# Chunked state-space scan with a gated feed-forward block: the second half of each chunk's y on exchanged PSUM column halves, copied out by two engines

## The chip, the cores and the metric

The kernel runs on one core of a Trainium2 chip. Its time is device microseconds of one launch; lower is better. The core has a matrix engine (TensorE, PE in the profile, its weight loads PEld), VectorE (DVE), ScalarE (ACT), GpSimd (POOL) and a queue engine that issues DMAs (SyncE, SP). They run side by side and wait for one another through semaphores. Each engine works through its instructions in program order. TensorE writes its results into PSUM; ScalarE and VectorE copy them from there into SBUF.

## What is computed

The reference is a chunked state-space scan (Mamba-2 style), followed by a feed-forward layer with the activation h·sigmoid(1.702·h). The core of the scan, per chunk:

```python
L = np.exp(cum[:, :, :, None] - cum[:, :, None, :]) * causal
M = np.einsum('bhin,bhjn->bhij', Cc, Bc) * L
y_intra = np.einsum('bhij,bhjd->bhid', M, xc)
y_inter = np.einsum('bhin,bhnd->bhid', Cc, state) * decay_to_i[:, :, :, None]
y[:, :, sl] = y_intra + y_inter
state = decay_full[:, :, None, None] * state + np.sum(Bx, axis=2)
...
h = x @ w_in                               # x is y, 3072 tokens x 256
out = (h / (1 + np.exp(-1.702 * h))) @ w_out   # 256 -> 2048 -> 256
```

There are 4 batches, 8 heads, 768 positions, 32 values per head and a state of 16 per head, all in fp32 on the chip.

## The kernel before

**Tiling.** The 3072 tokens are worked in six groups of 512 (numbers 0 to 5 in the code, "group one" to "group six" in the text). A group is four chunks of 128 positions, taken as two pairs of chunks. Each chunk of 128 is again two halves of 64 positions; the loop variable `i` is the half, `k` the chunk within a pair, `n` the pair.

**Making y.** `finish` computes y for a group in two steps. `inter` (line 821) multiplies the carried states with C: for each half `i` and each of four row strips `r` of 32 rows (two heads each), one matmul of 32 rows by 64 columns. `intra` (line 833) multiplies the masked, decayed scores with x: for each head and half one matmul of 64 rows by 32 columns, the half `i` choosing the upper or lower 64 rows. The position of a matmul on the array of 128 rows and 128 columns is `tile_position`; its columns are also the PSUM partitions of its result. Each fp32 matmul is two instructions in the profile, so a group has 128 of line 833 and 64 of line 821, or 56 where a batch begins in it and one state is zero.

The result is `y`, four PSUM banks: one for each half `i` and each tile `t` of 128 features (four heads of 32). The first group (`early`) has its own four banks and its own copies; groups two to six share one area of four banks (`area`, tag "cb", one buffer) with the scores `cb` and with the accumulators `acc`. That area is handed on in program order: scores, then y, then `acc` of the same round.

**Copying y.** ScalarE copies the two halves into `yT` in SBUF (line 860), with 128 partitions and 512 elements each.

**Using y.** `yT` of group two is used at once: `project_all(0)` computes the first group's output, with `finish` of group two between its steps, and `hidden(1, ...)` (line 889) follows. The later groups' `yT` is used a round later: `mix_y` (lines 913 to 915, VectorE) mixes its halves, since from group two on the feed-forward products are done by a seven-product scheme (Strassen-like): `first` (lines 945 to 955) for the first layer with PSUM results X and Y, copied and added by ScalarE (line 950) and VectorE (line 1077) into gT; `mix_g` mixes gT, and `product` (line 1050) accumulates the second layer in `acc`.

**Order.** All of it is one program written out by hand: strings such as `"2.T y refill 3.D 4.1 4.5 4.2 3.4 P P 4.6 P"` name the steps of a round in order, where `y` stands for `finish`, `3.D` for an addition on VectorE, `4.1` to `4.7` for products of the first layer and `P` for one of the second. `in_order` at the end fixes this order on each engine. `refill` sets off the loads for a later pair. `spread` (line 256) is the one of them that brings `a`, spread over the partitions, for the VectorE scan `decay` (line 402); it may be held back by a small memset on VectorE (line 253), behind which its DMAs stand on SP's queue.

Of the kernel before, what the change touches and what calls it, by code (L numbers as in the profile page):

```python
# [11 lines left out]
AF = mybir.ActivationFunctionType  # L12
# [23 lines left out]
def kernel(  # L36
# [31 lines left out]
    nc = tc.nc  # L68
# [4 lines left out]
    NB, NH, S, D = x.shape  # L73
# [5 lines left out]
    HB = NH // 2  # L79
# [7 lines left out]
    Q = NH // R  # L87
    H = P // 2
# [191 lines left out]
    early = const.tile([P, 1], FP32, name="early")  # L280
# [99 lines left out]
    for i, n, head in ((0, 1, PG), (1, 2, PG), (0, 0, 1)):  # L380
        t = whose[32 * i:32 * i + 32, n:n + 1]
# [14 lines left out]
    yT = {}  # L396
# [184 lines left out]
    def bank(name):  # L581
        return ps.tile([P, 4 * P], FP32, tag="ff", name=name)

    def area(name):
        return psa.tile([P, R, 4 * P], FP32, tag="cb", name=name)
# [202 lines left out]
    def finish(pairs, steps=range(2)):  # L788


        g, first = divmod(pairs[0], PG)
        early = pairs[0] < PG
        if 0 in steps:
            if early:
                y = [bank(f"y0_{i}")[:, :2 * P].rearrange("p (k i) -> p k i", i=H) for i in range(4)]
                begun_y[0] = [[y[2 * t + i] for t in range(NK)] for i in range(2)], set()
            else:
                both = area(f"y{pairs[0]}")[:, :, :len(pairs) * 2 * H].rearrange(
                    "p (s t) (k i) -> p s t k i", s=2, i=H)
                begun_y[pairs[0]] = [[both[:, i, t] for t in range(NK)] for i in range(2)] + [both], set()  # L800
        y, begun = begun_y[pairs[0]]

        def begin(i, t, parts):
            new = not begun & {(i, t, q) for q in parts}
            begun.update((i, t, q) for q in parts)
            return new

        def inter(n, p, ts=range(2)):

            for k in range(2):  # L810
                for i in range(2):
                    m = 2 * k + i
                    if (4 * p + m) % (2 * NC) == 0:
                        continue
                    old = state[p][:, m - 1] if m else state[p - 1][:, 3]
                    for r in range(R):
                        t = r // 2
                        if t not in ts:
                            continue
                        rows, to = slice(32 * r, 32 * r + 32), Q * D * (r % 2)  # L820
                        nc.tensor.matmul(  # L821
                            out=y[i][t][to:to + Q * D, 2 * n + k], lhsT=old[rows],
                            rhs=st[p]["CsT"][rows, k, SIDES[i]],
                            start=begin(i, t, range(Q * (r % 2), Q * (r % 2) + Q)), stop=early,
                            tile_position=(32 * r, to), skip_group_check=True)

        def intra(n, p):
            L = Ls[p]
            for k in range(2):
                for h in range(NH):  # L830
                    t, q = divmod(h, HB)
                    for i, side in enumerate(SIDES):
                        nc.tensor.matmul(  # L833
                            out=y[i][t][D * q:D * q + D, 2 * n + k], lhsT=rx[p][side, k, h],
                            rhs=L[side, k, h // Q, h % Q],
                            start=begin(i, t, (q,)), stop=not early, tile_position=(H * i, D * q),
                            skip_group_check=True)

        cols = slice(2 * first * P, 2 * (first + len(pairs)) * P)

        if first == 0:
            yT[g] = ffn.tile([P, NK, TG], FP32, tag="yT", name=f"yT{g}")
        if early:
            for n, p in enumerate(pairs):
                intra(n, p)
            for t in range(NK):
                for n, p in enumerate(pairs):
                    inter(n, p, (t,))
                for i in range(2):
                    nc.scalar.activation(  # L850
                        yT[g][:, t, cols].rearrange("p (k s i) -> p s k i", s=2, i=H)[:, i], y[i][t],
                        AF.Copy)
        else:
            for step in steps:
                for n, p in enumerate(pairs):
                    (inter, intra)[step](n, p)
            if 1 not in steps:
                return
            for i in range(2):
                nc.scalar.activation(  # L860
                    yT[g][:, :, cols].rearrange("p t (k s i) -> p s t k i", s=2, i=H)[:, i], y[2][:, i],
                    AF.Copy)
        for p in pairs:
            state.pop(p - 1, None)
            st.pop(p)
            Ls.pop(p)
# [234 lines left out]
    def turn_out(g, i):  # L1101

        t = out_tile(g, i).rearrange("p k e -> p (k e)")
        nc.vector.transpose(out=t, in_=sums[g][:, i].rearrange("p t e -> p (t e)"))
        rows = out[g * TG:(g + 1) * TG].rearrange("(b j) d -> j b d", j=32)
        for r in range(R):
            cols = slice(i * P + 32 * r, i * P + 32 * r + 32)
            nc.sync.dma_start(out=rows[:, :, cols],
                              in_=t[32 * r:32 * r + 32].rearrange("p (b e) -> p b e", e=32))
# [90 lines left out]
    keep_first()  # L1200
    dense(2)
    finish(range(PG))
    dense(0)
    join(0, 2)
# [25 lines left out]
    for i, k, c in ((2, 1, 1), (3, 2, 2), (4, 4, 4), (5, 6, 8), (6, 9, 12), (7, 12, 15)):  # L1230
# [3 lines left out]
    n, p = 2 * PG, 3 * PG  # L1234
# [7 lines left out]
    at(in_project[0], 9, lambda: score(pairs), lambda: gain(pairs), lambda: keep_both(pairs, True),  # L1242
       lambda: weigh(PG), lambda: weigh(PG + 1))
    at(in_project[0], 13, lambda: finish(pairs, (0,)))
    at(in_project[0], 15, lambda: finish(pairs, (1,)))
    at(in_project[0], 13, lambda: mix_in(1), lambda: mix_in(2), lambda: mix_in(3),
       lambda: turn_blocks(2), lambda: decay(n))
# [86 lines left out]
    k = NF // 2 - 1  # L1334
# [6 lines left out]
    for g in range(2, NG):  # L1341
        n, p = (g + 1) * PG, (g + 2) * PG
        more, most = g + 1 < NG, g + 2 < NG
        rows = [b for b in range(NB) if most and (g + 2) * CG <= b * NC < (g + 3) * CG]
# [32 lines left out]
        if more:  # L1377
# [4 lines left out]
                y=lambda: finish((n, n + 1)), refill=refill,  # L1382
# [6 lines left out]
        for j in range(5 if more else 4, NF // 2):  # L1389
            if j == 5:  # L1390
                do = lambda: (mix_g(g, 3), turn_out(g - 1, 0))
            else:
                do = lambda: mix_g(g, j - 2)
            run(g, steady(j, "o" if j == 6 else ""), seven(g, j - 4), M=do,
                o=lambda: turn_out(g - 1, 1))
# [6 lines left out]
        k = NF // 2 - 1  # L1402
# [42 lines left out]
```

## Time and profile before

| | |
|---|---|
| median of 3 runs | 350.76 us (350.66 to 352.0) |
| profiled execution | 349.68 us, of which 347.8 are the span of the core |
| granted TensorE clock | 1.000 |
| y, line 833 | 768 matmul instructions, median 216 ns each |
| y, line 821 | 352 matmul instructions, median 217 ns each |
| copies of y, line 860 | 10, median 592 ns each |

The span is the time from the first to the last instruction on the core; the rest of the execution lies around it. A line of the timeline gives start and length in us, the engine, the line of the kernel, the operation, the tile written and the tiles read, the sizes, the count of instructions merged into it and, in brackets, how long the engine stood idle before and what ended that. Matmuls overlap, so that the length of one is no measure of how fast they follow one another; that is read from their starts. PEld waits that end in a weight load are the waits of TensorE, because each matmul follows its load.

### The profile page before, as it was taken

The numbers are of one execution on the slowest core, as the hardware profiler recorded it, in microseconds if no ns is written. First come the engines' busy times: TensorE is split into PE (matmuls) and PEld (weight loads), VectorE is DVE, ScalarE is ACT, GpSimd is POOL, SyncE is SP. The second block draws the span as 40 slices with busy tenths as digits, with TensorE's granted clock in tenths as the row PEclk, the third lists the DMA queues.
The fourth block names the chain that finished last, engine by engine and source line by source line (L and its number), as shares of the span: only waits on it lengthen the run. The fifth ranks groups of instructions, "written<-read, shape, count | busy, mean of one in ns | idle before, by whom it ended". The sixth has DMA issues, their size and how long they took to land.

```text
span 347.8 us, 8141 instructions
## 1 busy us (share of the span) xinstructions
PE 342.0 (98%) x3392; PEld 271.9 (78%) x3392; DVE 253.5 (73%) x479; ACT 153.1 (44%) x349; POOL 12.9 (4%) x41
## 2 busy tenths in 40 slices
PE   8899999999999999999999999999999999999996
PEld 6644444557788888888888888888888888899996
DVE  5899999998679998839995649787555654455463
ACT  5698573107354324744332543442444321554320
POOL 8300000000000100000000000000000000000000
PEclk9999999999999999999999999999999999999999
DMA  6699997435526100435613036300000300000301
GB/s 162 142 336 193 283 212 155 81 77 93 105 58 128 33 2 15 63 104 102 101 28 50 2 81 117 64 2 1 2 2 2 61 2 0 0 2 0 62 0 61
DMA packets 89980, 25.92 MB, mean 75 GB/s; under 512 B 73432, under 2 KB 87128, under 8 KB 89944
## 3 DMA queue, kind: packets, MB, share of 16 engines
q1 hardware_dynamic: 89112, 24.88, 33.3%
q10 hardware_dynamic: 832, 0.52, 0.5%
q8 instruction: 26, 0.43, 0.5%
q14 instruction: 10, 0.08, 0.1%
HBM read 22.15 MB, written 3.24 MB: 73 GB/s over the span
## 4 chain that ended last, share of the span: by engine, by line
PE 97%; ACT 1%; DVE 1%; issue 0%; DVEq 0%
PE acc L1050 28%; PE X L945 20%; PE Y L955 14%; PE h L889 10%; PE o L987 8%; PE acc L1057 7%; PE y L833 2%; PE y L821 2%; PE cb L682 2%; PE A L713 1%; PE busy L440 1%; PE ab L554 1%; PE ab L548 0%; DVE steps L735 0%; ACT steps L730 0%; ACT drop L522 0%
## 5 line engine op out<-in xcount | busy, mean ns | idle before, releaser
L950 ACT ACTIVATE ac<-X 128x256 f32<-128x256 f32 x76 | 29.1, 383 | 78.6 <-PE X L945 78.2
L1050 PE MATMUL acc<-mg,mw 128*128 128x256 f32 x192 | 54.5, 379 | 0.0
L922 ACT ACTIVATE gT<-gT 128x512 f32<-128x512 f32 (+1 forms) x76 | 39.3, 520 | 34.1 <-DVE gT L1077 33.4
L1077 DVE TENSOR_TENSOR gT<-Y,ac 128x512 f32<-128x512 f32 x38 | 26.2, 689 | 36.1 <-PE Y L955 30.5
L945 PE MATMUL X<-my,mi 128*128 128x256 f32 x152 | 45.2, 380 | 0.0
L1077 DVE TENSOR_TENSOR gT<-Y,b 128x256 f32<-128x256 f32 x38 | 15.8, 419 | 35.2 <-PE Y L955 35.2
L1050 PEld LDWEIGHTS acc<-mg,mw 128*128 128x128 f32 x192 | 36.5, 190 | 5.0
L1050 PE MATMUL acc<-gT,w_out 128*128 128x256 f32 x128 | 35.5, 379 | 0.0
L889 PE MATMUL h<-yT,w_in 128*128 128x512 f32 (+2 forms) x98 | 35.5, 518 | 0.0
L945 PEld LDWEIGHTS X<-my,mi 128*128 128x128 f32 x152 | 28.0, 190 | 4.1 <-ACT ac L950 0.4
L889 PEld LDWEIGHTS h<-yT,w_in 128*128 128x128 f32 x98 | 17.0, 190 | 16.5 <-issue 14.3
L987 PE MATMUL o<-gT,w_out 128*128 128x512 f32 x64 | 28.6, 597 | 0.0
L913 DVE TENSOR_TENSOR mg<-gT 128x512 f32<-128x512 f32 x40 | 27.2, 681 | 0.0
L1050 PEld LDWEIGHTS acc<-gT,w_out 128*128 128x128 f32 x128 | 24.2, 190 | 3.4 <-ACT yT L860 0.2
L950 ACT ACTIVATE b<-X 128x256 f32<-128x256 f32 x38 | 14.6, 384 | 20.0 <-PE X L945 19.6
L945 PE MATMUL X<-yT,w_in 128*128 128x256 f32 x76 | 23.2, 389 | 0.0
L945 PE MATMUL X<-my,w_in 128*128 128x256 f32 x76 | 22.7, 382 | 0.2 <-issue 0.2
L955 PE MATMUL Y<-yT,w_in 128*128 128x256 f32 x76 | 22.7, 381 | 0.0
L955 PE MATMUL Y<-my,mi 128*128 128x256 f32 x76 | 22.6, 379 | 0.0
L955 PE MATMUL Y<-yT,mi 128*128 128x256 f32 x76 | 22.5, 379 | 0.0
L987 PEld LDWEIGHTS o<-gT,w_out 128*128 128x128 f32 x64 | 11.8, 190 | 13.2 <-issue 12.7
L402 DVE TENSOR_TENSOR_SCAN L<-a,idents 128x1024 f32<-128x1024 f32 x9 | 20.5, 2277 | 0.4 <-DMA a<-scratch 0.4
(156 smaller groups left out, 544.2 us busy)
## 6 DMA issues: line engine op xcount, KB each, us to landing
a<-scratch SPq DMA_DIRECT2D x18, 256.0 KB, 5.3
bits<-in_moe_w_out_dram SPq DMA_DIRECT2D x8, 512.0 KB, 5.4
x<-in_x_dram SPq DMA_DIRECT2D x24, 128.0 KB, 3.0
out_dram<-ob SPq DMA_DIRECT2D x40, 64.0 KB, 1.9
bits<-in_moe_w_in_dram SPq DMA_DIRECT2D x8, 256.0 KB, 4.6
bits<-in_moe_w_in_dram SPq DMA_DIRECT2D x4, 512.0 KB, 9.3
b<-in_B_dram SPq DMA_DIRECT2D x20, 64.0 KB, 3.0
af<-in_a_dram SPq DMA_DIRECT2D x3, 384.0 KB
```

Of the source, the lines that this page charges most:

```text
L402: nc.vector.tensor_tensor_scan(out=L, data0=ra[p].rearrange("p k e -> p (k e)"), data1=idents.rearrange("p h i -> p (h i)"), initial=0.0, ...
L682: nc.tensor.matmul(out=s["cb"][side, r, k].rearrange("p (q i) -> p q i", q=Q), lhsT=BT[rows, k, side], rhs=CT[rows, k, :, side], start=Tru ...
L889: nc.tensor.matmul(out=h[:, cols], lhsT=w_in[:, f, k], rhs=yT[g][:, k, cols], start=(k == 0 and e == 0), stop=(k == NK - 1), skip_group_ch ...
L913: nc.vector.tensor_tensor(out=t[:, 0:2], in0=B[:, :, 1], in1=B[:, 0], op=ALU.subtract)
L922: nc.scalar.activation(o, i, AF.Silu, scale=GELU_SCALE)
L945: nc.tensor.matmul(out=s["X"], lhsT=lhsT, rhs=rhs, start=i == "1", stop=i == "4", skip_group_check=True)
L950: nc.scalar.activation(copy, s["X"], AF.Copy)
L955: nc.tensor.matmul(out=o, lhsT=lhsT, rhs=rhs, start=s.pop("new", False), stop=i != "5", skip_group_check=True)
L987: nc.tensor.matmul(out=o[c], lhsT=w_out[:, c, f], rhs=gT[g, f // 2][:, f % 2], start=(f == 0), stop=(f == NF - 1), skip_group_check=True)
L1050: nc.tensor.matmul(out=acc[g][0][i][:, cols], lhsT=w, rhs=h[:, cols], start=(j == 0 and k == 0 and (i, 0) in begins), stop=(j == NF // 2 - ...
L1057: nc.tensor.matmul(out=o[k] if type(o) is list else o[:, cols], lhsT=h[:, cols], rhs=w, start=(j == 0 and (i, k) in begins), stop=(j == NF ...
L1077: nc.vector.tensor_tensor(out=o, in0=v, in1=w, op=ALU.add)
```

## The change

For groups two to six the second half `i` of each chunk puts its results on the other column half of the array, in both steps. In `inter` the 64 columns of a row strip are those of `r % 2` for the first half of a chunk and of the other value for the second. In `intra` the 32 columns of a head move by two strips for the second half. So in the PSUM banks of the second half, partitions 0 to 63 and 64 to 127 have changed places. The copy puts them back: the first half is copied by ScalarE as before; of the second, VectorE copies partitions 64 to 127 of y to 0 to 63 of yT, and ScalarE partitions 0 to 63 of y to 64 to 127 of yT. The first group (`early`) is as before. Lines after the change are three further down from the copy on.

```diff
@@ inter
                         t = r // 2
                         if t not in ts:
                             continue
-                        rows, to = slice(32 * r, 32 * r + 32), Q * D * (r % 2)
+                        half = r % 2 ^ (not early and i)
+                        rows, to = slice(32 * r, 32 * r + 32), Q * D * half
                         nc.tensor.matmul(
                             out=y[i][t][to:to + Q * D, 2 * n + k], lhsT=old[rows],
                             rhs=st[p]["CsT"][rows, k, SIDES[i]],
-                            start=begin(i, t, range(Q * (r % 2), Q * (r % 2) + Q)), stop=early,
+                            start=begin(i, t, range(Q * half, Q * half + Q)), stop=early,
                             tile_position=(32 * r, to), skip_group_check=True)
@@ intra
                 for h in range(NH):
-                    t, q = divmod(h, HB)
                     for i, side in enumerate(SIDES):
+                        t, q = divmod(h, HB)
+                        if i and not early:
+                            q = (q + Q) % HB
                         nc.tensor.matmul(
                             out=y[i][t][D * q:D * q + D, 2 * n + k], lhsT=rx[p][side, k, h],
@@ the copy
-            for i in range(2):
-                nc.scalar.activation(
-                    yT[g][:, :, cols].rearrange("p t (k s i) -> p s t k i", s=2, i=H)[:, i], y[2][:, i],
-                    AF.Copy)
+            o = yT[g][:, :, cols].rearrange("p t (k s i) -> p s t k i", s=2, i=H)
+            nc.scalar.activation(o[:, 0], y[2][:, 0], AF.Copy)
+            nc.vector.tensor_copy(o[:H, 1], y[2][H:, 1])
+            nc.scalar.activation(o[H:, 1], y[2][:H, 1], AF.Copy)
```

`Q` is 2 (heads per row strip), `D` 32, `HB` 4 (heads per tile of 128 features) and `H` 64.

## Prediction

> **What bounds the kernel now.** I read the page's shares and the chain that ended last first. Then I read the two matmul lines of y, the timeline around each of the five places where a y is made, and last the order of the changed program with the semaphore each instruction waits for.
>
> ```profile
> PE 342.0 (98%) x3392; PEld 271.9 (78%) x3392; DVE 253.5 (73%) x479; ACT 153.1 (44%) x349; POOL 12.9 (4%) x41
> PE 97%; ACT 1%; DVE 1%; issue 0%; DVEq 0%
> ```
>
> TensorE sets the time, at a granted clock of 1.000. What it stops doing is gained and what it waits is lost, unless a later wait takes it back. The state-space part is small: the two matmul lines of y are 2% of the chain each.
>
> ```profile
> 91.58 1.16 PE L821 MATMUL y<-CsT,S 32*64 32x64 f32 x64
> 96.76 1.48 PE L833 MATMUL y<-L,x 64*32 64x64 f32 x128
> 98.39 1.07 ACT L860 ACTIVATE yT<-y 128x512 f32<-128x512 f32 x2
> 99.50 0.73 PEld L1050 LDWEIGHTS acc<-gT,w_out 128*128 128x128 f32 x4 [0.18 <-ACT yT L860]
> 148.53 1.04 PE L821 MATMUL y<-CsT,S 32*64 32x64 f32 x56
> 180.12 0.79 PE L713 MATMUL A<-x,Be 64*32 64x64 f32 x56
> ```
>
> The first four lines are y of group three, its copy and what comes next. The two copies run one behind the other on ScalarE and end at 99.46; 0.04 later TensorE loads for `acc`, which lives in the PSUM area that y leaves. So here the copy has no slack. For groups four and five the copies end at 152.19 and 205.51 and the same load stands at 152.62 and 205.93, about 0.43 later. For group six they end at 258.88 and the load stands at 259.74, because TensorE itself lost 0.34 just before.
>
> **Part 1: `inter`.** Each matmul there uses 32 rows and 64 columns. Before, row strips 0 and 2 always use the left column half and 1 and 3 the right one, so four places of the array work. The records show four starts 6.7 ns apart, then the next four 58 ns after the first four. With the halves exchanged for the second half of a chunk, the eight matmuls of a chunk fall on eight places. The nearest row is L713, which has the same 64 moving columns on eight places: from its first matmul to the next stage it takes 0.72 for 56 (180.12 to 180.84) and 0.79 for 64. L821 takes 0.97 for 56 (148.53 to 149.50) and 1.09 for 64 (91.58 to 92.67). That is 0.25 and 0.30 less; its weight loads are twice as wide, so I take 0.23 and 0.28. Bounds: nothing at one end, half of the 0.83 and 0.94 between first and last start (0.41 and 0.47) at the other.
>
> A rule speaks against this gain. The Trainium skill, TensorE: Matmul & The Clock Gate, section "Wait — 56ns, not 53.3ns?", says that starts never come closer than about 25 ns however small the matmul. By it 56 matmuls would need 1.4 us and the exchange could bring nothing. The starts 6.7 ns apart in this trace contradict it for matmuls on separate places.
>
> **Part 2: `intra`.** It already covers eight places (two row halves, four column strips), and its first 32 starts stand 6.7 ns apart within each eight. The exchange permutes them: 0, bounded by ±0.1 a place, since L833 itself ranges from 1.41 to 1.50 first start to next stage.
>
> **Part 3: the copy.** In before, the second ScalarE copy starts 0.49 after the first (98.39, 98.86) and the pair takes 1.08. In the changed program the VectorE copy waits for a ScalarE semaphore, and the second ScalarE copy waits for a VectorE semaphore. The first copy is the only newer ScalarE work, so the three run strictly in turn. One ScalarE copy of 512 elements lasts 0.59; half the partitions leave the elements per partition alone. The VectorE copy is not in the trace. Its nearest row is L1077, which reads 512 PSUM elements in 0.69; the fast end is L480, VectorE on SBUF, 768 in 0.54, which with L341 (256 in 0.295) gives 0.42 for 512. I take 0.69. Hand-overs between engines measure 0.04 (98.03 to 98.06, 94.22 to 94.26). The chain is 0.59 + 0.04 + 0.69 + 0.04 + 0.59 = 1.95, against 1.08: **0.87 later** (0.60 with the fast copy).
>
> The Trainium skill, VectorE: DVE Perf Modes, section "Mode 2×_2P — use both read ports for one tensor", gives fp32 copies their double rate from SBUF only, since PSUM has one read port. By it the slow end is the right one, and the fast end would take 0.27 off every place.
>
> **What it meets, place by place.**
>
> Group two's first tile of work, `hidden(1, 0)`, needs all of yT. VectorE has the copy behind this queue:
>
> ```profile
> 77.13 2.22 DVE L402 TENSOR_TENSOR_SCAN L<-a,idents 128x1024 f32<-128x1024 f32 x1
> 78.47 1.09 ACT L860 ACTIVATE yT<-y 128x512 f32<-128x512 f32 x2 [11.39 <-PE y L833]
> 79.39 0.49 DVE L461 TENSOR_TENSOR Be<-b,L 128x128 f32<-128x128 f32 x2
> 79.80 2.29 DVE L402 TENSOR_TENSOR_SCAN L<-a,idents 128x1024 f32<-128x1024 f32 x1
> 80.19 3.68 PE L889 MATMUL h<-yT,w_in 128*128 128x128 f32 x24
> ```
>
> VectorE is 9.86 of 10 us busy from 70 to 80. The program puts the copy after `Be` and before the second scan, so it starts at 79.80 however early y is done, and the 0.23 of `inter` buys nothing here. It ends at 80.49, the last ScalarE copy at 81.12, the weight load starts at 81.17; a load that was waited for adds 0.11 (259.42: first matmul spaced 0.32, not 0.21). So 81.28 instead of 80.19: **+1.09**. The scan behind the copy slips 0.6, less than TensorE.
>
> Group three's y (the 98.39 lines): −0.28, then the area comes free 0.87 later. The load stood 0.06 before its matmul and now needs 0.11: +0.91. Net **+0.63**. Behind the copy on VectorE stand the two `mix_g`, and behind those a memset that gates the next DMA of `a` on SP's queue:
>
> ```profile
> 101.01 0.06 DVE L253 MEMSET a<- 128x1 f32 x1
> 101.10 1.27 SPq L256 DMA_DIRECT2D a<-scratch  x2
> 106.87 2.29 DVE L402 TENSOR_TENSOR_SCAN L<-a,idents 128x1024 f32<-128x1024 f32 x1 [0.37 <-DMA a<-scratch]
> 116.72 0.42 ACT L922 ACTIVATE gT<-gT 128x256 f32<-128x256 f32 x1 [2.71 <-DVE gT L1077]
> 117.05 0.37 ACT L950 ACTIVATE ac<-X 128x256 f32<-128x256 f32 x1
> 117.46 0.30 PEld L945 LDWEIGHTS X<-my,mi 128*128 128x128 f32 x2 [0.39 <-ACT ac L950]
> ```
>
> The scan already waits for that DMA; VectorE then works without a gap over 0.6 until 116.69, ScalarE waits for it, and TensorE at 117.46 waits for ScalarE. There is no slack in this row of waits. Before, VectorE began the first `mix_g` at 97.94, 0.30 before y's end at 98.24; now the copy ends 1.46 after y's end (copy one starts 0.15 after it, 0.58, 0.04, 0.69), and the `mix_g` begins 0.08 earlier than that. So the memset, the DMA and the scan slip 0.30 + 1.38 = 1.68 against y. TensorE has slipped 0.91 against y, so at 117.46 it waits another **+0.77**. The cover if I am wrong: a DMA that lands sooner than the 5.7 of before.
>
> Groups four and five's y (151.11 and 204.42): −0.23; the copies end 0.87 later, of which 0.38 was spare at the load after a 0.05 hand-over; the load stood 0.21 ahead of its matmul and needs 0.11. So +0.49 − 0.10 = +0.39, net **+0.16** each. The memset for `a` slips from 149.57 to about 152.4. The DMA landed 6.1 after it (155.7), so now at 158.6, before the scan at 159.60: covered by 1.0; the reads of C, B and x behind it on SP are wanted later still.
>
> Group six's y (257.80): −0.28; the load was 0.8 late already, so the delay just fits: **−0.28**.
>
> Sum: 1.09 + 0.63 + 0.77 + 0.16 + 0.16 − 0.28 = **+2.5**. The profiled execution takes 349.68 (347.8 of span and 1.88 around it), 1.1 under the median of 350.76. So 352.2 for such an execution and **353.3** on the median.
>
> **The rivals.**
>
> (a) *The late steps are cheaper.* `inter` at its halved end gives 0.18 or 0.19 more at four places (0.74), and the fast copy takes 0.27 off each of groups two to five and nothing of group six: 1.1. Together +0.7: 351.5. Either alone gives 351.9 to 352.6. Same within what can be told. For it: neither row is in the trace. Chance 0.22.
>
> (b) *Dearer.* `inter` gains nothing (+1.0) because issue, not the array, sets it. For it: L833 and L713 fall to about 8 ns a matmul after their first 32. Or the DMA of `a` in groups four and five lands 1 us after its scan. Then 354.3 to 355.3. Chance 0.12.
>
> (c) *Not slower.* The copies do not wait for each other in fact, because the semaphore values asked for are reached earlier; the place is the second ScalarE copy. Each y is then out 0.15 + 0.69 = 0.84 after its end against 1.22, no area is late, and the bill is the first place, where VectorE is still late (80.49 + 0.04 + 0.11 = 80.64, +0.45) less `inter` at 0.28 + 0.23 + 0.23 + 0.28, and what is left of the memset's slip in group three, 0 to 1.06 (0.84 less 0.08, and the 0.30): −0.6 to +0.5, so 350.2 to 351.3; with the halved `inter` down to 349.5. It decides when the VectorE copy begins before the first ScalarE copy ends. Against it: no other newer ScalarE work exists for that wait, and a y read straight after its matmuls would need TensorE's semaphore, which the VectorE copy does not ask for. Chance 0.06.
>
> **How the numbers follow.** My forecast has 0.60, the rivals 0.22, 0.12 and 0.06. A measurement here can tell about 0.5%, 1.75 us. Slower by more than that starts at 352.5: nearly all of the forecast's and of (b)'s cases, less the low edge of the forecast: 0.69. Within 0.5%: that edge, (a) and most of (c): 0.27. Faster: 0.04. The range reaches from (a)'s low side, 351.4, to the middle of (b), 354.9.
>
> **What would show it.** Right: L821's 56 matmuls in about 0.8 on the timeline instead of 1.04; per y one ScalarE copy, one VectorE copy, one ScalarE copy with no overlap, 1.9 to 2.0 together; the first `h` load of group two near 81.2 and naming the copy; a load for `acc` waiting about a microsecond in group three; the scan of 106.87 waiting longer for `a`. Wrong: the VectorE copy under way while the first ScalarE copy runs; L821 still 0.97; TensorE's waits at 80, 99 and 117 adding to less than 1 us.

## The result, and the profile after

The changed kernel takes 353.78 us (median of 15 runs, 352.24 to 357.37) against 350.66 us for the kernel before (15 runs). The ratio is 1.0102, interval 1.0078 to 1.0125. Measured again beside the later experiments it is 1.0068, interval 1.0043 to 1.0093 (353.67 against 351.38). The forecast was 353.3. The profiled execution takes 353.16 with a span of 351.3, at a granted clock of 1.000.

In the changed kernel `inter` is L822 and `intra` L836; from the copy on its line numbers are 3 higher: the copies L863 to L865, h L892, X L948, acc L1053.

The page of the changed kernel, the shares of the engines and the chain that ended last:

```profile
PE 342.7 (98%) x3392; PEld 270.6 (77%) x3392; DVE 257.3 (73%) x484; ACT 153.6 (44%) x349; POOL 13.0 (4%) x41
PE 75%; DVE 10%; DMA 7%; SPq 3%; ACT 2%; issue 2%; DVEq 0%
```

VectorE has 3.8 us more work: five copies of 0.69 (3.45) and a little scatter. The chain changes much more than the time does, from 97% TensorE to 75%. In time order it now runs, from the early loads up to 82 us, mostly through DMAs, SP's queue and VectorE (the DMA of `a` at 71, two transposes, the scan), and joins TensorE only at group two's h. Before, h waited for nothing, so the chain stayed on TensorE nearly all the way. A chain says through what the last work was released, not what an edit costs: the whole loss is about 3 us, under 1% of the span.

The timeline of group two:

```profile
78.20 2.23 DVE L402 TENSOR_TENSOR_SCAN L<-a,idents 128x1024 f32<-128x1024 f32 x1
79.16 0.60 ACT L863 ACTIVATE yT<-y 128x512 f32<-128x512 f32 x1 [11.34 <-PE y L836]
80.47 0.49 DVE L461 TENSOR_TENSOR Be<-b,L 128x128 f32<-128x128 f32 x2
80.99 0.69 DVE L864 COPY yT<-y 64x512 f32<-64x512 f32 x1
81.72 0.59 ACT L865 ACTIVATE yT<-y 64x512 f32<-64x512 f32 x1 [1.96 <-DVE yT L864]
82.36 0.74 PEld L892 LDWEIGHTS h<-yT,w_in 128*128 128x128 f32 x6 [2.15 <-ACT yT L865]
```

The three copies run in turn, the middle one waits behind the scan and `Be`, and the first weight load of h names the last copy. Of the 2.15 in its brackets, some is the ordinary wait of a load for the matmul stream; against the matmuls TensorE loses 1.48 here.

Group three's y, then group four's:

```profile
100.36 0.58 ACT L863 ACTIVATE yT<-y 128x512 f32<-128x512 f32 x1
100.97 0.69 DVE L864 COPY yT<-y 64x512 f32<-64x512 f32 x1 [0.97 <-ACT yT L863]
101.69 0.59 ACT L865 ACTIVATE yT<-y 64x512 f32<-64x512 f32 x1 [0.76 <-DVE yT L864]
102.33 0.73 PEld L1053 LDWEIGHTS acc<-gT,w_out 128*128 128x128 f32 x4 [1.03 <-ACT yT L865]
152.10 0.85 PE L822 MATMUL y<-CsT,S 32*64 32x64 f32 x56
156.39 0.73 PEld L1053 LDWEIGHTS acc<-gT,w_out 128*128 128x128 f32 x4 [0.51 <-ACT yT L865]
```

Copies of 0.58, 0.69 and 0.59 with hand-overs of 0.03 make 1.92 from 100.36 to 102.28; 0.05 later TensorE may load for `acc`. In group four the same chain meets 0.4 of slack and the load is held only 0.51. `inter`'s 56 matmuls take 0.85 on the timeline instead of 1.04.

And the row of waits that begins at the memset behind group three's copy:

```profile
104.65 0.06 DVE L253 MEMSET a<- 128x1 f32 x1
104.73 0.61 SPq L256 DMA_DIRECT2D a<-scratch  x1
110.45 2.29 DVE L402 TENSOR_TENSOR_SCAN L<-a,idents 128x1024 f32<-128x1024 f32 x1 [1.13 <-DMA a<-scratch]
113.64 0.42 ACT L925 ACTIVATE gT<-gT 128x256 f32<-128x256 f32 x1 [2.84 <-DVE gT L1080]
114.38 0.30 PEld L948 LDWEIGHTS X<-my,mi 128*128 128x128 f32 x2 [0.52 <-ACT ac L953]
121.03 0.30 PEld L948 LDWEIGHTS X<-my,mi 128*128 128x128 f32 x2 [0.75 <-ACT ac L953]
```

The memset is 3.64 later than before (101.01), TensorE at the same work 2.8 later. VectorE's scan waits 1.13 for `a` instead of 0.37. ScalarE waits for VectorE, and TensorE for ScalarE, at two places instead of one.

**An account by places.** All kernels here have the same 3,392 matmuls, nearly all in the same order. I matched their starts, in order, with the profiled execution of before. The first column is how late TensorE is at group two's last y matmul. The others are how much later it gets from place to place, and the last is their sum from that matmul to the end. All in us, one profiled execution per row.

| kernel | to y two | h two | to y three | y three | acc three | X, 111 | X, 117 | four | five | six | sum after y two |
|---|---|---|---|---|---|---|---|---|---|---|---|
| changed | 0.69 | 1.48 | 0.05 | -0.25 | 0.86 | 0.39 | 0.36 | 0.09 | 0.11 | -0.30 | **2.79** |
| changed, again | 2.23 | 1.46 | 0.01 | -0.25 | 0.85 | 0.45 | 0.36 | 0.10 | 0.11 | -0.10 | **3.01** |
| e1 ScalarE copies | 0.36 | 0.14 | 0.04 | -0.25 | 0.72 | 0 | -0.26 | 0.02 | 0.03 | 0.06 | **0.50** |
| e2 no exchange | 2.23 | 2.14 | 0.07 | 0 | 0.85 | 0.32 | 0.36 | 0.28 | 0.30 | -0.05 | **4.28** |
| e3 ScalarE in two | 1.84 | 0.14 | 0.15 | -0.24 | 0.85 | 0.61 | 0.36 | 0.09 | 0.11 | -0.29 | **1.79** |
| e4 ScalarE in three | 1.60 | 0.77 | 0.10 | -0.24 | 0.72 | 0 | -0.26 | 0.09 | 0.11 | -0.29 | **0.99** |
| e5 VectorE last | 2.93 | 0.26 | 0.10 | -0.25 | 0.84 | 1.26 | 0.36 | 0.07 | 0.09 | -0.31 | **2.42** |
| e6 `a` early | 0.77 | 1.90 | 0.06 | -0.25 | 0.86 | 0 | -0.26 | 0.09 | 0.11 | -0.29 | **2.22** |
| e7 copy before scan | 1.40 | 0.28 | 0.61 | -0.24 | 0.85 | 0.57 | 0.36 | 0.10 | 0.11 | -0.29 | **2.36** |
| e8 ScalarE, y earlier | 2.27 | 0 | -0.09 | -0.25 | 0.78 | 0 | -0.26 | 0.36 | 0.38 | -0.03 | **0.89** |
| e9 before, y earlier | 3.63 | 0 | -0.09 | 0 | -0.04 | 0 | -0.26 | -0.09 | -0.07 | -0.40 | **-0.95** |
| e9, again | 2.26 | 0 | -0.05 | 0 | -0.04 | 0 | -0.26 | -0.09 | -0.07 | -0.43 | **-0.93** |
| e10 e3 and e6 | 1.73 | 0.14 | 0.13 | -0.25 | 0.85 | 0 | -0.26 | 0.09 | 0.11 | -0.30 | **0.55** |

The first column is not the change. Up to group two's y the copies are those of before, yet it runs from 0.4 to 3.6. It is highest for e9, where group two is that of before to the last instruction. TensorE is already late by 0.1 to 1.0 at 12 us, while the first loads arrive. In several executions group two's `intra` also takes 0.4 to 1.8 longer than its usual 1.41, because TensorE stands still in its middle, where the profile names no releaser. So the execution of before that I worked from was an early one, and single times differ by several us for reasons that no edit has. What stands behind that column repeats to a few hundredths in most places. The exceptions are h two, which is explained below, X of 111, where the scan starts 5.74 to 6.05 after the memset, depending on when the DMA of `a` lands, and once group six (-0.10). The columns of groups four and five stand 0.09 and 0.07 too low in every row: in the execution of before `intra` took 1.50 and 1.49 there, against 1.41 in every kernel that makes y at the same place, e2 without the exchange among them. Here one pair of executions says more than a difference of medians.

### The profile page after: what moved, and what is told of

Its sections match the earlier page's. It is cut to its first block, busy times and chain, and to the rows that moved or that the text cites. A ratio compares the mean times of both kernels' runs of the same rounds, so it can differ in the third digit from the quotient of the medians.

```text
span 351.3 us, 8140 instructions
## 1 busy us (share of the span) xinstructions
PE 342.7 (98%) x3392; PEld 270.6 (77%) x3392; DVE 257.3 (73%) x484; ACT 153.6 (44%) x349; POOL 13.0 (4%) x41
## 4 chain that ended last, share of the span: by engine, by line
PE 75%; DVE 10%; DMA 7%; SPq 3%; ACT 2%; issue 2%; DVEq 0%
PE acc L1053 28%; PE X L948 18%; PE Y L958 13%; PE acc L1060 7%; DMA a<-scratch 4%; PE h L892 2%; PE cb L682 2%; DVE p L222 2%; DMA bits<-in_moe_w_in_dram 1%; DVE m L208 1%; SPq L124 1%; DMA bits<-in_moe_w_out_dram 1%; PE y L836 1%; DVE p L192 1%; SPq L150 1%
## 5 line engine op out<-in xcount | busy, mean ns | idle before, releaser
L1053 PE MATMUL acc<-mg,mw 128*128 128x256 f32 x192 | 54.5, 379 | 0.0
L948 PE MATMUL X<-my,mi 128*128 128x256 f32 x152 | 45.3, 381 | 0.5 <-ACT ac L953 0.3
L1053 PEld LDWEIGHTS acc<-mg,mw 128*128 128x128 f32 x192 | 36.5, 190 | 5.0
L892 PE MATMUL h<-yT,w_in 128*128 128x512 f32 (+2 forms) x98 | 35.7, 519 | 1.4 <-ACT yT L865 1.3
L1053 PE MATMUL acc<-gT,w_out 128*128 128x256 f32 x128 | 35.9, 382 | 1.0 <-ACT yT L865 0.6
L948 PEld LDWEIGHTS X<-my,mi 128*128 128x128 f32 x152 | 27.9, 190 | 4.9 <-ACT ac L953 1.3
L892 PEld LDWEIGHTS h<-yT,w_in 128*128 128x128 f32 x98 | 17.0, 190 | 18.4 <-issue 13.9
L1053 PEld LDWEIGHTS acc<-gT,w_out 128*128 128x128 f32 x128 | 24.0, 190 | 5.7 <-ACT yT L865 2.6
L948 PE MATMUL X<-yT,w_in 128*128 128x256 f32 x76 | 23.2, 389 | 0.0
L948 PE MATMUL X<-my,w_in 128*128 128x256 f32 x76 | 22.6, 381 | 0.0
```

The lines of the kernel that those rows point to most:

```text
L892: nc.tensor.matmul(out=h[:, cols], lhsT=w_in[:, f, k], rhs=yT[g][:, k, cols], start=(k == 0 and e == 0), stop=(k == NK - 1), skip_group_ch ...
L948: nc.tensor.matmul(out=s["X"], lhsT=lhsT, rhs=rhs, start=i == "1", stop=i == "4", skip_group_check=True)
L1053: nc.tensor.matmul(out=acc[g][0][i][:, cols], lhsT=w, rhs=h[:, cols], start=(j == 0 and k == 0 and (i, 0) in begins), stop=(j == NF // 2 - ...
```

## The experiments

Each was timed in 5 rounds beside the kernel before. That kernel's median was 350.8 with e1 to e4, 351.17 with e5, e6, e8 and e9, and 351.38 with e7, e10 and the repeats.

**e1: ScalarE makes all three copies**

```diff
-            nc.vector.tensor_copy(o[:H, 1], y[2][H:, 1])
+            nc.scalar.activation(o[:H, 1], y[2][H:, 1], AF.Copy)
```

> The exchange as in the change, but all three copies by ScalarE in a row (two of 64 partitions for the second half), none by VectorE. Theory A (the time is lost through the copy on VectorE: its place in VectorE's queue in group two, and three copies strictly in turn): the copies take about 0.6 + 0.5 + 0.5 = 1.6 us per y; in group two the first h follows without a wait; in group three the acc load waits about half a microsecond and the DMA of a no longer slips; inter keeps its 0.78 and 0.84 to the next stage. Net of about -0.8 us against before: 349.9 (349.0 to 350.8). Rival B (the exchanged positions themselves cost time on TensorE): still 1 to 3 us slower than before.

Measured: 351.15 (350.0 to 352.17), ratio 1.0007 [0.9991, 1.0023]. The loss is gone, so it sat in VectorE's copy and not in the exchange. The time is above the expected range: the gain I expected isn't there. The timeline of e1 in group three shows why:

```profile
98.68 0.58 ACT L863 ACTIVATE yT<-y 128x512 f32<-128x512 f32 x1
99.27 0.60 ACT L864 ACTIVATE yT<-y 64x512 f32<-64x512 f32 x1
99.88 0.59 ACT L865 ACTIVATE yT<-y 64x512 f32<-64x512 f32 x1
100.52 0.73 PEld L1053 LDWEIGHTS acc<-gT,w_out 128*128 128x128 f32 x4 [0.89 <-ACT yT L865]
```

The copies start 0.59 and 0.61 apart, where the two of before started 0.47 apart. Three take 1.79 from first start to last end, so the third costs 0.72 at `acc`, more than `inter` saves.

**e2: the split copy without the exchange**

```diff
-                        half = r % 2 ^ (not early and i)
+                        half = r % 2
...
-            nc.vector.tensor_copy(o[:H, 1], y[2][H:, 1])
-            nc.scalar.activation(o[H:, 1], y[2][:H, 1], AF.Copy)
+            nc.vector.tensor_copy(o[:H, 1], y[2][:H, 1])
+            nc.scalar.activation(o[H:, 1], y[2][H:, 1], AF.Copy)
```

(`intra`'s line for `q` goes too.)

> Both steps of y on the old column halves, only the copy of the second half split between VectorE and ScalarE, 64 partitions each, straight across. Theory A: the same chain of copies without what inter gains at four places (0.20 + 0.25 + 0.20 + 0.25 = 0.9), so about 4 us slower than before: 354.6 (353.5 to 356.5); L821 back at 0.97 and 1.09 to the next stage. Rival B (the exchange itself costs): faster than the changed kernel, below 353.3.

Measured: 356.18 (354.52 to 356.69), ratio 1.0137 [1.0109, 1.0165]. In the account the places of `inter` show the exchange's worth: y three 0 instead of -0.25, and groups four, five and six 0.19, 0.19 and 0.25 dearer. So the exchange does save 0.2 to 0.25 a group. e2's larger loss at h two (2.14) is not due to it: VectorE's scan started 0.07 after y's last matmul in this execution, 0.71 ahead of it in that of the changed kernel, and the sum given below for h makes 2.26 of that.

**e3: ScalarE makes the middle copy in group two alone**

```diff
-            nc.vector.tensor_copy(o[:H, 1], y[2][H:, 1])
+            if g == 1:
+                nc.scalar.activation(o[:H, 1], y[2][H:, 1], AF.Copy)
+            else:
+                nc.vector.tensor_copy(o[:H, 1], y[2][H:, 1])
```

> The changed kernel, but in group two alone the VectorE copy is made by ScalarE. Theory A with C (in group two the copy passes on however late VectorE is by then, and that lateness comes from the loads of the weights and differs from run to run): 1.6 to 1.8 us of the 3.1 are gone, 352.0 (351.3 to 352.6), and the runs lie closer together than the 352.2 to 357.4 of the changed kernel. Without C: 1.1 to 1.3 gone, 352.6, and the same spread. Rival B: no change, 353.8.

Measured: 352.84 (352.47 to 354.65), ratio 1.0061 [1.004, 1.0083]. About 0.9 of the 3.1 is gone, less than either form of the theory expected. By the account h two loses 0.14 instead of 1.48, but X of 111 loses 0.61 instead of 0.39, because the scan starts 6.03 after the memset here and 5.80 in the changed kernel. Whether the times lie closer together for the reason given (C) stays open.

**e4: the same in group three alone** (`if g == 2`)

> The changed kernel, but in group three alone the VectorE copy is made by ScalarE. Theory A: the acc load waits about 0.5 us instead of 1.0, the memset and the DMA of a are 1.7 us earlier against y, and the wait at the X of product 7.6 (about 121 us in) goes; 1.4 to 1.6 us of the 3.1 are gone, 352.2 (351.5 to 353.0). If only the acc load counts and the DMA of a does not: 0.4 to 0.5 gone, 353.3. Rival B: no change.

Measured: 352.51 (351.75 to 354.17), ratio 1.0047 [1.0025, 1.0068]. e3 and e4 lay the loss at two places: without VectorE's copy h two costs 0.14 instead of 1.48, and in group three X costs -0.26 instead of 0.75. The load for `acc` hardly changes (0.72 against 0.86), since three ScalarE copies are about as long as the mixed three.

**e5: VectorE's copy last**

```diff
-            nc.vector.tensor_copy(o[:H, 1], y[2][H:, 1])
             nc.scalar.activation(o[H:, 1], y[2][:H, 1], AF.Copy)
+            nc.vector.tensor_copy(o[:H, 1], y[2][H:, 1])
```

> The changed kernel with the three copies in another order: ScalarE, ScalarE, then VectorE. Theory (the copies run in turn, and each place pays for what stands behind them): the chain becomes 0.49 + 0.59 + 0.04 + 0.69 = 1.8 instead of 1.95. Group two: VectorE's copy still starts behind its scan, but no ScalarE copy follows it, so the first load of h is 0.6 earlier against TensorE than in the changed kernel (shift there +1.0 instead of +1.6). Group three: the load for acc 0.15 earlier, but VectorE is held 0.45 longer before its mix_g, so the wait at X (121 us) grows by about 0.35 net. Groups four and five 0.15 earlier each. Sum -0.6 - 0.15 + 0.35 - 0.3 = -0.7: 353.1 (352.3 to 353.8). Rival (the VectorE copy costs its own 0.7 on TensorE's path wherever it stands, and the queue behind it does not matter): no growth at X, every place 0.15 earlier, 352.5 or less.

Measured: 354.48 (352.3 to 355.03), ratio 1.0093 [1.0065, 1.0122]: outside the theory's range and no better than the changed kernel. The wait at X grew from 0.75 to 1.62, which is 0.87 where 0.35 was expected. The memset stands 5.26 behind y's last matmul instead of 4.65, so it slips by a whole ScalarE copy (0.61) more; the other 0.25 is the DMA, since the scan starts 6.05 after the memset instead of 5.80. From the timeline:

```profile
102.65 0.69 DVE L865 COPY yT<-y 64x512 f32<-64x512 f32 x1 [1.57 <-ACT yT L864]
103.39 0.73 PEld L1053 LDWEIGHTS acc<-gT,w_out 128*128 128x128 f32 x4 [1.02 <-DVE yT L865]
106.33 0.06 DVE L253 MEMSET a<- 128x1 f32 x1
```

The rival (only the copy's own 0.7 counts, not what stands behind it) is refuted by that growth. The 0.26 at h two of this execution isn't to be compared, because y itself stood 1.5 there without a named cause and VectorE caught up meanwhile.

**e6: in group three, the loads of `a` ahead of y**

```diff
-    run(1, "... 3.S 3.3 2.T 3.T y",
-        ..., W=lambda: mix_w(0))
+    run(1, "... 3.S 3.3 2.T 3.T L y",
+        ..., W=lambda: mix_w(0), L=lambda: more_loads())
...
-    run(1, "4.1 4.5 4.2 P P 4.6 P L P 4.7 P P P 4.D", seven(1, 0), L=more_loads)
+    run(1, "4.1 4.5 4.2 P P 4.6 P P 4.7 P P P 4.D", seven(1, 0))
```

> The changed kernel with one move in group three alone: the memset and the DMA of a (and the loads behind them) are put ahead of y instead of behind it, so that on VectorE the memset stands before the copy and the two mix_g. Theory (part of the loss in group three is the memset that slips behind the VectorE copy, then the DMA of a, then the scan, then the wait of X at 121 us): that wait goes, the 0.29 that the kernel before lost there goes with it, and the load for acc at 102 us stays as late as in the changed kernel. Time 353.8 - 0.5 to 0.9: 353.1 (352.6 to 353.5). Rival (the wait at X comes from the acc load and from VectorE's added 0.69 of work, not from the DMA): unchanged, 353.8 (353.4 to 354.2).

Measured: 352.77 (351.79 to 354.79), ratio 1.0059 [1.0038, 1.008].

```profile
100.46 0.06 DVE L253 MEMSET a<- 128x1 f32 x1
101.48 0.69 DVE L864 COPY yT<-y 64x512 f32<-64x512 f32 x1 [0.96 <-ACT yT L863]
102.85 0.73 PEld L1053 LDWEIGHTS acc<-gT,w_out 128*128 128x128 f32 x4 [1.03 <-ACT yT L865]
120.44 0.41 PEld L948 LDWEIGHTS X<-my,mi 128*128 128x128 f32 x2
```

VectorE's copy and the load for `acc` are as late as in the changed kernel (1.03 in the brackets in both). Only the memset stands ahead, and X waits for nothing: 0 and -0.26 in place of 0.39 and 0.36. This shows that the path from the memset over the DMA and the scan to TensorE is the cause of that term.

**e7: in group two, VectorE's copy ahead of the scan**

```diff
-       lambda: turn_blocks(2), lambda: decay(n))
+       lambda: turn_blocks(2))
...
-    at(in_project[0], 15, lambda: finish(pairs, (1,)))
+    at(in_project[0], 15, lambda: finish(pairs, (1,)), lambda: decay(n))
```

> The changed kernel with one move in group two alone: the first scan (and its Be) is put behind y instead of ahead of it, so VectorE's copy no longer stands behind the scan. Theory (h of group two is late because the copy waits in VectorE's queue: in the runs so far h starts 4.16 us after that scan starts, or 1.97 after y's last matmul, whichever is later): the copy starts about 0.9 after y's last matmul, h about 2.3 after it, so the loss at h is 0.3 to 0.4 instead of 1.6. Both scans then run 1 to 1.5 later than in the changed kernel, and some of it is given back at the second A (0.6) or at y of group three. Net -0.3 to -1.2: 353.0 (352.5 to 353.6). Rival (the loss at h is the copy's own 0.7 and the two hand-overs, the queue adds nothing): h stays 1.5 or more late, 353.8 or more.

Measured: 353.89 (353.44 to 355.09), above the expected range, ratio 1.0064 [1.004, 1.0088], not to be told from the changed kernel beside it (1.0068). The profile does show the mechanism:

```profile
80.50 0.69 DVE L864 COPY yT<-y 64x512 f32<-64x512 f32 x1 [1.58 <-ACT yT L863]
81.12 2.28 DVE L402 TENSOR_TENSOR_SCAN L<-a,idents 128x1024 f32<-128x1024 f32 x1
81.87 3.38 PEld L892 LDWEIGHTS h<-yT,w_in 128*128 128x128 f32 x24 [0.95 <-ACT yT L865]
86.50 0.36 PEld L713 LDWEIGHTS A<-x,Be 64*32 64x32 f32 x24 [0.61 <-DVE Be L461]
```

h loses 0.28 instead of 1.48, but the scan behind it makes the second `A` wait: 0.61 comes back there, and X at 111 waits 0.57. So VectorE's queue is the cause at h, and moving the copy inside that queue passes part of the delay on. By the account 0.4 should be left as a gain; the times don't show it, and whether it is real stays open.

**e8: ScalarE's copies, group two as before, y and the loads of `a` earlier**

```diff
-            nc.vector.tensor_copy(o[:H, 1], y[2][H:, 1])
-            nc.scalar.activation(o[H:, 1], y[2][:H, 1], AF.Copy)
+            if g == 1:
+                nc.scalar.activation(o[:, 1], y[2][:, 1], AF.Copy)
+            else:
+                nc.scalar.activation(o[:H, 1], y[2][H:, 1], AF.Copy)
+                nc.scalar.activation(o[H:, 1], y[2][:H, 1], AF.Copy)
...
-    "... 3.S 3.3 2.T 3.T y"
+    "... 3.S 3.3 L y 2.T 3.T"
...
-                "... 3.5 3.2 3.7 2.T y "
+                "... 3.5 3.2 y 3.7 2.T "
```

(The exchange itself is limited to groups three to six.)

> A version meant to keep the gain: the three copies of the exchange all by ScalarE (as in the run with ScalarE's copies), groups three to six exchanged and group two as in the kernel before, y moved two products earlier (0.86 us) in groups three to six so that the longer copy is covered, and the loads of a in group three ahead of y. Theory (inter gains 0.2 to 0.25 a group and the third copy took it back at the acc load): -0.25 - 0.2 - 0.2 - 0.25 on inter, -0.2 and -0.3 for the two small stalls of the kernel before (117.5 and 259.4 us), so -1.4: 349.3 (348.8 to 350.2). Rival (inter's gain never reaches the end, or ScalarE's longer queue becomes late for the ac operations): 350.4 to 351.4.

Measured: 352.27 (351.24 to 353.61), ratio 1.0038 [1.0022, 1.0054]: a miss. The move was smaller than I had written. `2.T` and `3.T` hold no matmul, so y came one product earlier (0.43) in groups four to six and not at all in group three. And in groups four to six a new wait took the place of the one at `acc`:

```profile
154.05 0.59 ACT L868 ACTIVATE yT<-y 64x512 f32<-64x512 f32 x1
154.67 0.38 ACT L956 ACTIVATE ac<-X 128x256 f32<-128x256 f32 x1
155.10 0.30 PEld L951 LDWEIGHTS X<-my,w_in 128*128 128x128 f32 x2 [0.78 <-ACT ac L956]
```

The `ac` that frees an X stands behind the third copy in ScalarE's queue.

**e9: the control, the kernel before with the same moves and no exchange** (the last two hunks of e8's diff)

> Control for the version with ScalarE's copies and an earlier y: the kernel before, with no exchange and its two copies, with the same moves of y and of the loads of a. Theory: only the two small stalls go (117.5 us 0.3, 259.4 us 0.34), so -0.5: 350.2 (349.7 to 350.8), and the version with the exchange is 0.5 to 1.0 faster than this one. Rival (the exchange gives nothing that lasts): both the same within 0.3.

Measured: 350.76 (349.22 to 352.37), ratio 0.9979 [0.9955, 1.0003]. Run again:

> The control once more, to settle its sign: the kernel before with no exchange, with only the loads of a put ahead of y in group three and y one product earlier in groups four to six. By its profile the two small stalls are gone (0.25 and 0.34): 350.3 (349.8 to 350.7) against 350.9 of the kernel before on this chip. If the first result was chance: within 0.1% of it.

Measured: 350.18 (349.17 to 350.99), ratio 0.9954 [0.9932, 0.9976], against 351.38. The first interval still touches 1, the second is clear of it. This is the version that beats both kernels, and it has no exchange.

```profile
119.26 0.41 PEld L945 LDWEIGHTS X<-my,mi 128*128 128x128 f32 x2
260.64 0.41 PEld L945 LDWEIGHTS X<-my,w_in 128*128 128x128 f32 x2
```

These are the loads that stood waiting at 117.46 and 259.42 in the kernel before; neither has a wait now. Of the account's -0.95, 0.26 and about 0.4 are these two; 0.16 of the rest is the slow `intra` of the execution of before. Against e9, e8 is 1.8 dearer after y two (0.89 against -0.94): with these moves the exchange and its third copy lose more than `inter` wins.

**e10: e3 and e6 together**

> The changed kernel with both of VectorE's queue effects taken away: in group two ScalarE does the middle copy, and in group three the memset and the DMA of a stand ahead of y. If the account is complete, what is left against the kernel before is +0.15 at h, +0.75 at the load for acc of group three, about 0 at X, +0.15 each in groups four and five, less inter's 0.15 to 0.3 a group and the 0.3 stall of group six: +0.3 in all, 351.0 (350.5 to 351.8). If something else of the VectorE copy costs (its 0.69 of added work at five places, or memory contention), 352.0 or more.

Measured: 352.24 (350.86 to 354.28), ratio 1.0013 [0.9993, 1.0033]. The time is above the range, but the kernel before was 0.6 above its first median in this set too. Against it the medians make +0.9 and the ratio +0.5, where +0.3 was expected, and the account has +0.55. With VectorE's two queue effects gone, nothing of size is left but the loads for `acc` (0.85 in group three, 0.38 in each later group), which `inter` pays for in part. VectorE's copies in groups four to six cost nothing beyond that.

**The changed kernel again**

> The changed kernel again, so that the two others of this call can be compared with it on the same chip and day: 353.8 (353.0 to 354.5).

Measured: 353.67 (352.93 to 356.7), ratio 1.0068 [1.0043, 1.0093].

## Why the prediction was right

**Part 1, `inter`.** Right in kind, and mis-sized by 0.03. From its first matmul to the next stage it takes 0.775 for 56 and 0.843 for 64, against 0.973 and 1.090: 0.20 and 0.25 saved, where 0.23 and 0.28 were taken from L713. The first 32 starts come in eights, 7 ns apart; the second eight begins 107 ns after the first, the others 58 to 59 ns after one another. From the 33rd matmul on the starts stand 4 to 17 ns apart, 13 on average in a row of 56. So the 25 ns between starts, which the prediction set against this gain, doesn't hold for these matmuls. The 8 ns that rival (b) took from the later matmuls of L833 and L713 was a misreading: they stand 10 ns apart on average in L833 and 11 to 18 in L713.

**Part 2, `intra`.** 1.41 at four places, which is what e2 has without the exchange. In group two it took 1.55, but e9, with the old group two, took 2.71 there once and 1.41 the other time, and e1, e3 and e4, with the exchange, 1.41. So no cost of the exchange shows.

**Part 3, the copy.** Strictly in turn. VectorE's copy takes 0.69, the end that I took. The chain is 1.92 against a forecast of 1.95 (and the pair of before takes 1.07 in group three, not the 1.08 set against it), the load for `acc` loses 0.86 against 0.91, and y three with it 0.61 against 0.63.

**Group two.** This is the mis-sized term: 1.09 forecast, 1.48 and 1.46 measured. The mechanism is right, but the number hung on one execution. In the changed kernel h starts 4.16 after the scan starts (78.20 to 82.36); without a wait it starts 1.97 after y's last matmul (78.22 to 80.19 before). So the loss is 2.19 + (scan's start - y's last matmul). With the times of before (77.13 - 78.22) this gives 1.10. In the changed kernel it gives 2.19 + 78.20 - 78.91 = 1.48, in its second execution 2.19 + 79.71 - 80.45 = 1.45, in e4 2.19 + 78.40 - 79.82 = 0.77, in e6 2.19 + 78.69 - 78.99 = 1.89; measured are 1.48, 1.46, 0.77 and 1.90. The scan's lead over y depends on how late VectorE is against TensorE, and that differs from execution to execution. One source shows in the waits: near 53 us VectorE waits for the DMA of the second layer's weights (L192), 0.2 in the execution of before, 0.7 and 1.7 in the two of the changed kernel, 2.5 in e2's. I should have put a spread on this term.

**Group three's memset.** 0.77 forecast at one place; 0.39 + 0.36 = 0.75 measured, at two (111 and 117). e6 shows that the path is the one named. Without the slip these places stand at 0 and -0.26, so the full price is 1.0: the kernel before already lost 0.26 there.

**Groups four to six.** 0.16, 0.16 and -0.28 forecast; 0.09, 0.11 and -0.30 measured (once -0.10). In groups four and five the terms hold: the load for `acc` loses 0.38 against 0.39, `inter` saves 0.20 against 0.23, and the rest is the slow `intra` of the execution of before. In group six the number is right by luck. The delay was to fit behind the late load for `acc` at no cost, with the small stall ahead of it left as it was. In fact the stall went and the load waited:

```profile
259.42 0.30 PEld L945 LDWEIGHTS X<-my,w_in 128*128 128x128 f32 x2 [0.56 <-ACT ac L950]
262.40 0.41 PEld L948 LDWEIGHTS X<-my,w_in 128*128 128x128 f32 x2
263.32 0.30 PEld L1053 LDWEIGHTS acc<-gT,w_out 128*128 128x128 f32 x2 [0.51 <-ACT yT L865]
```

The first line is of the kernel before, the others of the changed one. By the matched starts that is -0.43 at X, +0.38 at `acc` and -0.25 in `inter`. No run separates why the stall goes.

**The sum.** 2.5 forecast, 2.8 and 3.0 in the account; the term at h alone is 0.4 above its forecast. The medians moved by 3.1 and 2.3. Of the rivals, (a) needed a VectorE copy at its fast end or an `inter` that saves twice as much (and its own terms give 352.2 to 352.6 for either alone, not 351.9), (b) an `inter` that gains nothing or a DMA of `a` that comes too late in groups four and five, (c) copies that don't wait; the lines and the account above contradict each. As forecast, the exchange has no price in itself. It saves about 0.9 in groups three to six (e2 against the changed kernel: 0.25, 0.19, 0.19 and 0.25), and the split copy loses it several times over. Why the copies wait for one another was not tested. That both engines read the same PSUM tile is the likely reason. That both write the same SBUF tile is less likely: at 15.49 us of the profile before, ScalarE (L743) and VectorE (L744) start together, read one tile `steps` and write different parts of one tile `S`. A y in two tiles, which would test the first, was not tried.

## What to carry to other kernels

Cost an instruction on a busy engine by what stands ahead of it in that engine's queue and what stands behind it, down to memsets that gate a DMA; its own 0.69 was the smaller part of the bill. A copy that hands work between engines in turn is as long as the sum of its parts, so splitting it helps only where the parts can overlap. Before a saving of 0.2 a stage is bought with an instruction of 0.6 elsewhere, look for stalls that a mere reordering removes: here two moves without any exchange gave 0.2% (not clear of noise) and 0.5% in two measurements.

## What the runs showed of the hardware

- Copies on ScalarE alone start 0.47 to 0.50 apart when each has 128 partitions on the same partitions in and out, and 0.59 to 0.61 apart in e1, where the second and third have 64 partitions and move them to the other half. A copy lasts 0.59 in either form: half the partitions save nothing. Which of the differences sets the wider spacing wasn't separated.
- 56 matmuls of 32 rows by 64 columns take 0.775 on eight places of the array against 0.973 on four, 64 of them 0.843 against 1.090.
- VectorE's copy of 64 partitions by 512 elements from PSUM takes 0.69, as much as its additions of 128 by 512.
- An execution's early lateness (0.4 to 3.6 us at group two's y) passes through to the end: the two of e9 are 1.37 apart there and 1.35 at their last matmul. A profile of one execution gives the price of a place well, and the total time badly.
